# Attention and channel mix on one core: natural 128-token loads, contiguous evacuation, mixing spread over slots

## The chip, the cores and the metric

The kernel runs on one core of one Trainium2 chip. The metric is the time of one execution on the device in microseconds (us). The engines are named as in the profile: PE is TensorE with its weight loads as PEld, DVE is VectorE, ACT is ScalarE, POOL is GpSimd, and SP is SyncE, which here only issues transfers.

## The reference, cut to what matters

Eight batches of eight heads, 576 tokens, head size 64. Attention is causal by blocks of 64 tokens; its output, heads side by side, is the input x (8 x 576 x 512) of a channel mix with two mixed copies of x and three weight matrices.

```
scores = q @ k.T / 8 ; masked where block(i) < block(j)      # blocks of 64 tokens
attn   = softmax(scores) ; x = (attn @ v) as (8, 576, 512)
x_prev = x shifted by one token, zero ahead of each batch
xk = mu_k * x + (1 - mu_k) * x_prev ; xr = mu_r * x + (1 - mu_r) * x_prev
k  = relu(xk @ w_k) ; v = (k * k) @ w_v ; r = sigmoid(xr @ w_r)
out = r * v
```

## The kernel before, in words

**Loads.** `load_qk` (L82) loads q and k of a batch with SP: each of 96 partitions gets six consecutive tokens of a head, so one row of a transfer is 6 x 256 B = 1536 B. Four LD buffers hold one batch. `load_v` (L104) loads v in tiles of 128 tokens with rows of 256 B, three buffers. POOL casts q and k to bf16 (`cast_qk`, L93, tile QKN) and v to f16 (`cast_v`, L112, tile VO). The three weight matrices come as transfers that POOL issues (`load_w`, L135).

**Attention.** A pair of heads fills 128 partitions. `qk_transpose` (L145) turns q and k of a pair with six PE transposes of 96 tokens each into a PSUM tile PQK. The six pieces lie there by remainder of the token, so the copy out reads PSUM with a step of 96 elements: ACT copies q to QT (L161), DVE copies k to KT (L164). `score` (L177) computes three tiles of scores of a pair, ACT exponentiates them into E (L189), POOL zeroes masked corners (L191). `av_norm` (L218) multiplies E with v (PA) and DVE normalises (Rc L230, X L231).

**Channel mix.** `x_transpose` (L237) turns x by PE (PX), ACT copies it to XT (L259), in chunks of 512 tokens: there are 9 chunks for 8 batches. `mix` (L266) does for each of the four 128-channel groups of a chunk: POOL subtracts neighbouring tokens into DT (L272, two buffers) and mends the column where a batch begins (L277); DVE makes XK and XR (L280). `pk`, `prr` and `pv` are the three products: PK goes through ACT (relu, KR) and DVE (square, K), PR through ACT (tanh, T), PV through DVE (OV, L315), and SP stores OV.

**Order.** Work is put into slots, 13 for a batch, and the work of one slot on attention is interleaved with the units `pk`, `prr`, `pv` of an earlier chunk. `mix` of chunk b stands as a whole in slot 5 of the next batch; the units of that chunk begin two slots later. A scheduler behind this still moves instructions of one engine past each other where their inputs allow. All PSUM tiles but the scores share one pool of four buffers (`ps_m`), and every engine works through its queue in order. The lines that decide are these:

```
at(s0 + NP_ + 5, mix, b)
first = (c + 1) * NP_ + 7 if c < NCH - 1 else B * NP_ + 7
```

Of the kernel before, what the change touches and what calls it, by code (L numbers as in the profile page):

```python
# [17 lines left out]
def kernel(  # L18
# [17 lines left out]
    HP = H // 2  # L36
    CCn = C // P
    JCn = DF // P
    R = 6
    PQ = S // R  # L40
    D1 = D + 1
    CH = 512
    NCH = B * S // CH
# [16 lines left out]
    d_pool = pool("dp", 2)  # L60
    xk_pool = pool("xk", 2)
    kr_pool = pool("kr", 3)
    k2_pool = pool("k2", 1)
# [14 lines left out]
    QN, KN, QT, KT = {}, {}, {}, {}  # L78

    LD = {}  # L80

    def load_qk(b):  # L82
        for hh in range(2):
            for n, src in enumerate((q, k)):
                LD[b, n, hh] = ld_pool.tile([PQ, HP, R, D], FP, tag="ld",
                                            name="LD")
                for h in range(0, HP, 2):
                    nc.sync.dma_start(  # L88
                        LD[b, n, hh][:, h:h + 2],
                        src[b, hh * HP + h:hh * HP + h + 2].rearrange(  # L90
                            "h (p r) d -> p h r d", r=R))

    def cast_qk(b, hh, h):  # L93
        for n, (dst, tag) in enumerate(((QN, "qn"), (KN, "kn"))):
            if h == 0:
                dst[b, hh] = qk_pool.tile([PQ, R, HP, D], BF, tag=tag, bufs=2,
                                          name="QKN")
            nc.gpsimd.tensor_copy(  # L98
                dst[b, hh][:, :, h:h + 2].rearrange("p r h d -> p h r d"),
                LD[b, n, hh][:, h:h + 2])  # L100
# [15 lines left out]
    load_qk(0)  # L116
    for pr in range(HP):
        cast_qk(0, pr // 2, pr % 2 * 2)
# [24 lines left out]


    def qk_transpose(b, pr):  # L145
        if pr == 0:
            QT[b] = tr_pool.tile([P, HP, S], BF, tag="qt", name="QT")
            KT[b] = tr_pool.tile([P, HP * S + D], BF, tag="kt", name="KT")
            nc.vector.memset(KT[b][:, HP * S:], 0.0)
        for which in range(2):  # L150
            N = (QN, KN)[which][b, pr // 2]
            pst = ps_m.tile([P, CH], FP, tag="m", name="PQK")[:, :].bitcast(BF)
            view = pst[:, 0:S].rearrange("p (r t) -> p t r", r=R)
            for r in range(R):
                nc.tensor.matmul(  # L155
                    pst[:, r * PQ:(r + 1) * PQ], N[:, r, pr % 2 * 2:pr % 2 * 2 + 2, :].rearrange(
                        "p h d -> p (h d)"),
                    identb[0:PQ, 0:PQ], is_transpose=True,
                    start=(r == 0), stop=(r == R - 1))
            if which == 0:  # L160
                nc.scalar.copy(  # L161
                    QT[b][:, pr].rearrange("p (t r) -> p t r", r=R), view)
            else:
                nc.vector.tensor_copy(  # L164
                    KT[b][:, pr * S:(pr + 1) * S].rearrange(
                        "p (t r) -> p t r", r=R), view)
# [96 lines left out]

    XKR = {}

    def mix(c):  # L266
        x = XT[c]
        XK = xk_pool.tile([P, CCn, CH], F16, tag="xk", name="XK")
        XR = xk_pool.tile([P, CCn, CH], F16, tag="xr", name="XR")
        for cc in range(CCn):  # L270
            DT = d_pool.tile([P, CH], FP, tag="d", name="DT")
            nc.gpsimd.tensor_tensor(DT, x[:, cc, 1:CH + 1], x[:, cc, 0:CH],  # L272
                                    ALU.subtract)
            for b in range(B):
                t = b * S - c * CH
                if 0 <= t < CH:
                    nc.gpsimd.tensor_copy(DT[:, t:t + 1],  # L277
                                          x[:, cc, t + 1:t + 2])
            for (dst, mu) in ((XK, MUK), (XR, MUR)):
                nc.vector.scalar_tensor_tensor(  # L280
                    dst[:, cc], DT, mu[:, cc:cc + 1],
                    x[:, cc, 1:CH + 1], ALU.mult, ALU.add)
        XKR[c] = (XK, XR)
# [40 lines left out]
    def at(slot, fn, *args):  # L324
        slots.setdefault(slot, []).append((fn, args))

    for b in range(B):
        s0 = b * NP_
        order = [("s", 0, 0), ("s", 0, 1), ("s", 0, 2), ("l",)] + [
            ("s", pr, i) for pr in range(1, HP) for i in range(3)]  # L330
        for n, o in enumerate(order):
            if o[0] == "l":
                at(s0 + n, score_last, b)
            else:
                at(s0 + n, score, b, o[1], o[2])
            if b + 1 < B:
                if n == 0:
                    at(s0, load_qk, b + 1)
                if n in (3, 5, 7, 9):
                    at(s0 + n, cast_qk, b + 1, (n - 3) // 4, (n - 3) % 4)  # L340
                if n == 3 and b == 0:
                    at(s0 + n, load_w)
                if n == 4:
                    at(s0 + n, load_v, b + 1)
                if n in (8, 9, 10, 11, 12):
                    at(s0 + n, cast_v, b + 1, n - 8)
                if n in (6, 8, 10, 12):
                    at(s0 + n, qk_transpose, b + 1, (n - 6) // 2)
# [66 lines left out]
```

## Time and profile before

| what | us |
|---|---|
| median of 3 runs | 352.56 (351.91 to 353.87) |
| the profiled execution | 352.34 |
| its span | 350.6 |
| PE busy | 289.2 (83% of the span) |
| DVE busy | 212.8 (61%) |
| ACT busy | 197.0 (56%) |
| POOL busy | 161.4 (46%) |

The span is what the profiler saw of the engines; 1.74 us of the execution lie around it. The mean granted clock of PE over the span is 0.941 of full speed. The line of DMA engines in the page stands near full only in about the first sixth of the span.

### The profile page before, as it was taken

Reading aid. Unit: us, or ns where it says so; the run is one execution under the profiler, and the core shown is the slowest. Engines: PE = TensorE matmul, PEld = TensorE weight load, DVE = VectorE, ACT = ScalarE, POOL = GpSimd, SP = SyncE. Lnnn points to the kernel's source line nnn. Section 1 sums busy time; section 2 is a strip of 40 time slices with the busy share of each in tenths; the row PEclk is TensorE's granted clock in tenths of the full one; section 3 lists DMA queues with packets and bytes.
Section 4 is the critical chain, followed back from the end, with each engine's and each line's share of the span. In section 5 each row is a group of like instructions: output and inputs, shape, how many; then the busy total and the mean of one; then the engine's idle time right before and its main releaser. Section 6 shows DMA issues by size and latency. Waiting matters only on the chain.

```text
span 350.6 us, 6713 instructions
## 1 busy us (share of the span) xinstructions
PE 289.2 (83%) x2608; PEld 155.6 (44%) x2608; DVE 212.8 (61%) x366; ACT 197.0 (56%) x289; POOL 161.4 (46%) x311
## 2 busy tenths in 40 slices
PE   2750784889939996999699959997999999849995
PEld 1320652445515553555345535554455546414442
DVE  2202558982577629762967286828673974996452
ACT  2750683476716673876468636865695684315250
POOL 5811959855645754564545563665013512640000
PEclk9999995899958998999879998999899999998999
DMA  8999788095559483159104930030000100000302
GB/s 219 220 197 258 173 208 198 19 263 151 153 168 262 139 216 92 50 150 267 52 15 138 275 81 32 2 105 32 30 2 32 61 33 32 30 31 33 120 15 104
DMA packets 59184, 40.81 MB, mean 116 GB/s; under 512 B 40208, under 2 KB 54032, under 8 KB 59152
## 3 DMA queue, kind: packets, MB, share of 16 engines
q1 hardware_dynamic: 57056, 37.76, 39.6%
q0 software_dynamic: 2096, 2.62, 4.4%
q8 instruction: 20, 0.33, 0.4%
q14 instruction: 12, 0.10, 0.1%
HBM read 33.56 MB, written 9.44 MB: 123 GB/s over the span
## 4 chain that ended last, share of the span: by engine, by line
PE 56%; DVE 14%; POOL 11%; DMA 7%; issue 4%; ACT 4%; SPq 2%; POOLq 0%; DVEq 0%; ACTq 0%
PE PK L292 20%; PE PV L312 10%; PE PR L302 8%; PE PA L225 7%; POOL DT L272 6%; DMA LD<-in_k_dram 6%; DVE XR L280 5%; PE PS L185 5%; DVE XK L280 4%; PE PQK L155 3%; SPq L88 2%; DVE OV L315 2%; POOL QKN L98 2%; ACT E L189 2%; PE PX L243 2%
## 5 line engine op out<-in xcount | busy, mean ns | idle before, releaser
L189 ACT ACTIVATE E<-PS 128x1024 f16<-128x1024 f32 x96 | 97.0, 1028 | 41.0 <-PE PS L185 25.1
L292 PE MATMUL PK<-XK,WK 128*128 128x512 f16 x288 | 81.5, 427 | 18.7 <-DVE OV L315 16.7
L297 DVE TENSOR_TENSOR K<-KR 128x512 f16<-128x512 f32 x72 | 56.8, 801 | 25.7 <-ACT KR L296 25.0
L296 ACT ACTIVATE KR<-PK 128x512 f32<-128x512 f32 x72 | 43.0, 600 | 52.2 <-PE PK L292 43.9
L98 POOL CAST QKN<-LD 96x768 bf16<-96x768 f32 x64 | 58.5, 944 | 23.3 <-PE PQK L155 7.4
L312 PE MATMUL PV<-WV,K 128*128 128x512 f16 x288 | 67.8, 379 | 0.0
L191 POOL MEMSET E<- 64x128 f16 x128 | 22.9, 200 | 79.6 <-ACT E L189 73.9
L272 POOL TENSOR_TENSOR DT<-XT 128x512 f32<-128x512 f32 x36 | 42.4, 1186 | 25.4 <-DVE XR L280 14.1
L292 PEld LDWEIGHTS <-WK 128*128 128x128 f16 x288 | 27.5, 106 | 58.7 <-issue 39.0
L225 PE MATMUL PA<-VO,E 128*128 128x65 f16 x896 | 39.6, 197 | 10.5 <-DVE X L231 5.2
L315 DVE SCALAR_TENSOR_TENSOR OV<-T,PV 128x512 f32<-128x512 f32 x36 | 24.5, 680 | 35.5 <-PE PV L312 35.5
L225 PEld LDWEIGHTS <-E 128*128 128x128 f16 x896 | 35.0, 100 | 22.0 <-issue 8.3
L185 PE MATMUL PS<-QT,KT 64*128 64x512 bf16 (+4 forms) x320 | 41.9, 322 | 3.3 <-ACT E L189 3.1
L155 PE MATMUL PQK<-identb,QKN 96*128 96x96 bf16 x384 | 27.2, 223 | 18.8 <-POOL QKN L98 16.7
L280 DVE SCALAR_TENSOR_TENSOR XK<-DT,MUK,XT 128x512 f16<-128x512 f32 x36 | 30.6, 851 | 18.2 <-POOL DT L277 17.7
L312 PEld LDWEIGHTS <-K 128*128 128x128 f16 x288 | 27.2, 98 | 28.8 <-issue 1.1
L280 DVE SCALAR_TENSOR_TENSOR XR<-DT,MUR,XT 128x512 f16<-128x512 f32 x36 | 38.4, 1067 | 0.0
L302 PE MATMUL PR<-WR,XR 128*128 128x512 f16 x144 | 37.0, 382 | 1.3 <-DVE KT L164 1.3
L155 PEld LDWEIGHTS <-QKN 96*128 96x128 bf16 x384 | 22.2, 106 | 32.1 <-POOL QKN L98 23.0
L114 POOL CAST VO<-VL 128x512 f16<-128x512 f32 (+1 forms) x40 | 25.6, 655 | 21.9 <-DMA VL<-in_v_dram 17.6
L305 ACT ACTIVATE T<-PR 128x512 f32<-128x512 f32 x36 | 21.5, 596 | 21.0 <-PE PR L302 21.0
L231 DVE TENSOR_TENSOR X<-PA,Rc 128x320 f32<-128x320 f32 x64 | 31.2, 489 | 1.7
(35 smaller groups left out, 198.3 us busy)
## 6 DMA issues: line engine op xcount, KB each, us to landing
LD<-in_q_dram SPq DMA_DIRECT2D x32, 288.0 KB, 4.1
LD<-in_k_dram SPq DMA_DIRECT2D x32, 288.0 KB, 5.2
out_dram<-OV SPq DMA_DIRECT2D x36, 256.0 KB, 2.0
VL<-in_v_dram SPq DMA_DIRECT2D x32, 256.0 KB, 4.9
WK<-in_moe_w_k_dram POOLq DMA_DIRECT2D x1, 1024.0 KB, 10.1
VL<-in_v_dram SPq DMA_DIRECT2D x8, 128.0 KB, 4.1
WV<-in_moe_w_v_dram POOLq DMA_DIRECT2D x1, 1024.0 KB, 16.0
WR<-in_moe_w_r_dram POOLq DMA_DIRECT2D x1, 512.0 KB, 10.2
```

The costliest lines, as they stand in the source:

```text
L98: nc.gpsimd.tensor_copy(dst[b, hh][:, :, h:h + 2].rearrange("p r h d -> p h r d"), LD[b, n, hh][:, h:h + 2])
L155: nc.tensor.matmul(pst[:, r * PQ:(r + 1) * PQ], N[:, r, pr % 2 * 2:pr % 2 * 2 + 2, :].rearrange("p h d -> p (h d)"), identb[0:PQ, 0:PQ], i ...
L185: nc.tensor.matmul(PS[:, h, col:col + n], KT[b][rows, pr * S + kc * P: pr * S + (kc + 1) * P], QT[b][rows, pr, q0:q0 + n], start=True, sto ...
L189: nc.scalar.activation(E[:, :, i, :], PS, AF.Exp, scale=ISQ)
L225: nc.tensor.matmul(PA[:, m * D1:(m + 1) * D1], stationary(b, h, kc, m), VO[:, kc, h, 0:D1], start=(kc == 0), stop=(kc == m))
L272: nc.gpsimd.tensor_tensor(DT, x[:, cc, 1:CH + 1], x[:, cc, 0:CH], ALU.subtract)
L280: nc.vector.scalar_tensor_tensor(dst[:, cc], DT, mu[:, cc:cc + 1], x[:, cc, 1:CH + 1], ALU.mult, ALU.add)
L292: nc.tensor.matmul(ps, WK[:, cc, jc * P:(jc + 1) * P], XKR[c][0][:, cc], start=(cc == 0), stop=(cc == CCn - 1))
L296: nc.scalar.activation(KR, ps, AF.Relu)
L297: nc.vector.tensor_tensor(K2[c][:, jc], KR, KR, ALU.mult)
L302: nc.tensor.matmul(ps, XKR[c][1][:, cc, jt * P:(jt + 1) * P], WR[:, cc], start=(cc == 0), stop=(cc == CCn - 1))
L312: nc.tensor.matmul(ps, K2[c][:, jc, jt * P:(jt + 1) * P], WV[:, jc], start=(jc == 0), stop=(jc == JCn - 1))
```

## The change

Loads: q and k of a pair of heads come as four tiles of 128 tokens in rows of 256 B, one transfer for each head and tensor; the last 64 tokens of all heads come apart, q on the upper and k on the lower 64 partitions of one tile TL. There are eight LD buffers and five for v. POOL casts them to NB and TB. Transposes: eight full 128 x 128 transposes for a pair go into one PSUM bank, four more for a batch's tails; DVE alone copies them out, 1024 neighbouring elements at a time, into one tile QKT, and ACT no longer takes part. Mixing: the four subtractions of a chunk stand together (`mix_d`) with a DT for the whole chunk and one mending copy; the eight DVE instructions follow two per slot over the next four slots, all of XK first; the units of the chunk begin two slots later than before. E has two buffers instead of three.

```diff
-    qk_pool = pool("qk", 1)
+    ld_pool = pool("ld", 8)
+    vl_pool = pool("vl", 5)
+    qk_pool = pool("qk", 5)
+    tl_pool = pool("tl", 2)
     tr_pool = pool("tr", 2)
-    e_pool = pool("ep", 3)
+    e_pool = pool("ep", 2)
-    ld_pool = pool("ld", 4)
-    vl_pool = pool("vl", 3)
-    d_pool = pool("dp", 2)
+    d_pool = pool("dp", 1)
...
+    def load_qk(b, pr):
+        for n, src in enumerate((q, k)):
+            LD[b, pr, n] = ld_pool.tile([P, 4, 2, D], FP, tag="ld", name="LD")
+            for h in range(2):
+                nc.sync.dma_start(
+                    LD[b, pr, n][:, :, h],
+                    src[b, 2 * pr + h, 0:512].rearrange("(t p) d -> p t d",
+                                                        p=P))
+    def load_tail(b):
+        TL[b] = tl_pool.tile([P, H, D], FP, tag="tl", name="TL")
+        for n, src in enumerate((q, k)):
+            nc.sync.dma_start(TL[b][n * D:n * D + D],
+                              src[b, :, 512:576].rearrange("h p d -> p h d"))
+    def cast_qk(b, pr):
+        NB[b, pr] = qk_pool.tile([P, 2, 4, P], BF, tag="nb", name="NB")
+        for n in range(2):
             nc.gpsimd.tensor_copy(
+                NB[b, pr][:, n],
+                LD[b, pr, n][:, :].rearrange("p t h d -> p t (h d)"))
...
+        pst = ps_m.tile([P, CH], FP, tag="m", name="PQK")[:, :].bitcast(BF)
+        n = 8 if pr < HP else HP
+        for i in range(n):
+            src = (NB[b, pr][:, i // 4, i % 4] if pr < HP
+                   else NB[b, HP][:, i * P:(i + 1) * P])
+            nc.tensor.matmul(pst[:, i * P:(i + 1) * P], src, identb,
+                             is_transpose=True, start=(i == 0),
+                             stop=(i == n - 1))
+        if pr < HP:
+            nc.vector.tensor_copy(
+                QKT[b][:, :, pr * S:pr * S + 512],
+                pst.rearrange("p (n t) -> p n t", n=2))
...
-    def mix(c):
+    def mix_d(c):
         x = XT[c]
+        DT = d_pool.tile([P, CCn, CH], FP, tag="d", name="DT")
...
         for cc in range(CCn):
+            nc.gpsimd.tensor_tensor(DT[:, cc], x[:, cc, 1:CH + 1],
+                                    x[:, cc, 0:CH], ALU.subtract)
+        for b in range(B):
+            t = b * S - c * CH
+            if 0 <= t < CH:
+                nc.gpsimd.tensor_copy(DT[:, :, t:t + 1], x[:, :, t + 1:t + 2])
+    def mix(c, n, cc):
+        nc.vector.scalar_tensor_tensor(
+            XKR[c][n][:, cc], XKR[c][2][:, cc], (MUK, MUR)[n][:, cc:cc + 1],
+            XT[c][:, cc, 1:CH + 1], ALU.mult, ALU.add)
...
-        at(s0 + NP_ + 5, mix, b)
-    at(B * NP_ + 5, mix, NCH - 1)
+        sm = s0 + NP_ + 5
+        for c in ((b,) if b < B - 1 else (b, b + 1)):
+            sm = s0 + NP_ + 5 + 6 * (c - b)
+            at(sm, mix_d, c)
+            for i in range(8):
+                at(sm + 1 + i // 2, mix, c, i // 4, i % 4)
...
-        first = (c + 1) * NP_ + 7 if c < NCH - 1 else B * NP_ + 7
+        first = (c + 1) * NP_ + 9
```

On POOL, at the start of the program, the order of the casts and of the three weight transfers (WK, WR, WV) before is this; QKN is a cast of q or k, VO one of v, E the zeroing of masked corners:

```order
11 L98 CAST QKN<-LD 96x2x6x64 x8
12 L136 DMA WK<-in_moe_w_k_dram 128x4x1024
13 L114 CAST VO_116<-VL 128x8x64 x3
14 L191 MEMSET E 64x2x64 x4
15 L137 DMA WR<-in_moe_w_r_dram 128x4x512
16 L98 CAST QKN<-LD 96x2x6x64
17 L138 DMA WV<-in_moe_w_v_dram 128x8x512
```

And now:

```order
11 L98 CAST NB<-LD 128x512 x2
12 L104 CAST TB<-TL 128x512
13 L146 DMA WK<-in_moe_w_k_dram 128x4x1024
14 L98 CAST NB<-LD 128x512 x2
15 L147 DMA WR<-in_moe_w_r_dram 128x4x512
16 L98 CAST NB<-LD 128x512 x2
17 L200 MEMSET E 64x2x64 x4
18 L148 DMA WV<-in_moe_w_v_dram 128x8x512
```

The first weight transfer was issued behind all eight casts of batch 0; now it is issued behind the casts of its first pair and the tail.

On DVE, in the middle of the program where a chunk is mixed while the next batch's attention runs, the order before is this; XK and XR are the mixed copies, OV the product that goes out, Rc and X the normalisation, KT a copy of transposed k:

```order
143 L257 COPY XT<-XT 128x4
144 L280 SCALAR_TENSOR_TENSOR XK<-DT,MUK,XT 128x512
145 L280 SCALAR_TENSOR_TENSOR XR<-DT,MUR,XT 128x512
146 L280 SCALAR_TENSOR_TENSOR XK<-DT,MUK,XT 128x512
147 L315 SCALAR_TENSOR_TENSOR OV<-T,PV 128x512
148 L280 SCALAR_TENSOR_TENSOR XR<-DT,MUR,XT 128x512
149 L280 SCALAR_TENSOR_TENSOR XK<-DT,MUK,XT 128x512
150 L280 SCALAR_TENSOR_TENSOR XR<-DT,MUR,XT 128x512
151 L280 SCALAR_TENSOR_TENSOR XK<-DT,MUK,XT 128x512
152 L280 SCALAR_TENSOR_TENSOR XR<-DT,MUR,XT 128x512
153 L230 RECIPROCAL Rc<-PA 128x5
154 L315 SCALAR_TENSOR_TENSOR OV<-T,PV 128x512
```

And now, with QKT as the copy of transposed q and k:

```order
149 L290 SCALAR_TENSOR_TENSOR XK<-DT,MUK,XT 128x512 x4
150 L290 SCALAR_TENSOR_TENSOR XR<-DT,MUR,XT 128x512
151 L324 SCALAR_TENSOR_TENSOR OV<-T,PV 128x512
152 L290 SCALAR_TENSOR_TENSOR XR<-DT,MUR,XT 128x512
153 L239 RECIPROCAL Rc<-PA 128x5
154 L290 SCALAR_TENSOR_TENSOR XR<-DT,MUR,XT 128x512
155 L240 TENSOR_TENSOR X<-PA,Rc 128x5x64
156 L290 SCALAR_TENSOR_TENSOR XR<-DT,MUR,XT 128x512
157 L239 RECIPROCAL Rc<-PA 128x5
158 L240 TENSOR_TENSOR X<-PA,Rc 128x5x64
159 L324 SCALAR_TENSOR_TENSOR OV<-T,PV 128x512
160 L168 COPY QKT<-PQK 128x2x512
```

The four XK now stand first and together, the last three XR between one OV and two normalisations that stood behind all eight.

On POOL, where a chunk in the middle is mixed, the order before is this (VO is a cast of v, DT the subtraction and its mending copy):

```order
113 L272 TENSOR_TENSOR DT<-XT 128x512 x2
114 L277 COPY DT<-XT 128x1 x2
115 L191 MEMSET E 64x2x64
116 L272 TENSOR_TENSOR DT<-XT 128x512
117 L277 COPY DT<-XT 128x1
118 L191 MEMSET E 64x2x64
119 L272 TENSOR_TENSOR DT<-XT 128x512
120 L277 COPY DT<-XT 128x1
```

And now:

```order
112 L200 MEMSET E 64x2x64 x3
113 L104 CAST TB<-TL 128x512
114 L282 TENSOR_TENSOR DT<-XT 128x512 x4
115 L119 CAST VO_120<-VL 128x8x64
116 L287 COPY DT<-XT 128x4
```

The four subtractions now stand together, and one cast of v stands between them and the mending copy.

## Rows read from the trace of the kernel before

**Rows 1.** Stretches of the span: start:end, length, busy us (instructions) by engine, clock, DMA, GB/s

```profile
0.00:44.00 44.00, 21.12 (x243) 12.91 (x244) 11.99 (x31) 19.02 (x23) 22.99 (x51) 1.00 0.99 213
44.00:60.00 16.00, 9.78 (x128) 6.62 (x125) 11.08 (x16) 10.73 (x15) 11.81 (x23) 0.78 0.94 222
60.00:102.00 42.00, 33.25 (x321) 18.09 (x319) 29.31 (x46) 23.55 (x35) 28.12 (x51) 0.91 0.54 142
102.00:211.00 109.00, 99.05 (x933) 53.81 (x932) 70.42 (x128) 67.88 (x100) 57.73 (x107) 0.92 0.53 146
211.00:280.00 69.00, 65.65 (x635) 35.28 (x632) 46.35 (x84) 47.46 (x69) 27.81 (x61) 0.96 0.11 36
280.00:316.00 36.00, 29.67 (x230) 15.41 (x231) 28.36 (x46) 15.85 (x27) 12.95 (x20) 1.00 0.09 33
316.00:346.50 30.50, 30.50 (x135) 13.47 (x133) 14.62 (x23) 12.54 (x21) 0.00 (x0) 0.95 0.16 61
```

**Rows 2.** Timeline, 127.5 to 139 us: start, us, engine, line, out<-in, [idle before <-releaser]

```profile
127.91 2.04 POOL L272 TENSOR_TENSOR DT<-XT 128x512 f32<-128x512 f32 x2 [1.37 <-ACT XT L259]
130.11 0.75 DVE L280 SCALAR_TENSOR_TENSOR XK<-DT,MUK,XT 128x512 f16<-128x512 f32 x1 [2.08 <-POOL DT L277]
...
133.11 0.68 PE L155 MATMUL PQK<-identb,QKN 96*128 96x96 bf16 x12
...
134.00 1.42 POOL L272 TENSOR_TENSOR DT<-XT 128x512 f32<-128x512 f32 x1 [0.51 <-DVE XR L280]
134.44 1.52 DVE L280 SCALAR_TENSOR_TENSOR XR<-DT,MUR,XT 128x512 f16<-128x512 f32 x1
...
138.18 1.37 PE L292 MATMUL PK<-XK,WK 128*128 128x512 f16 x3 [2.99 <-DVE OV L315]
```

**Rows 3.** The seven stretches with a lowered clock; columns as in Rows 1

```profile
53.00:64.00 11.00, 6.94 (x47) 3.58 (x47) 9.90 (x14) 2.59 (x5) 10.14 (x19) 0.54 0.66 148
97.00:108.00 11.00, 6.31 (x36) 3.02 (x36) 7.41 (x13) 2.53 (x5) 3.50 (x9) 0.53 0.70 200
138.00:142.00 4.00, 3.83 (x10) 1.19 (x10) 2.48 (x6) 0.89 (x2) 0.00 (x0) 0.57 0.17 66
172.00:180.00 8.00, 6.01 (x28) 2.16 (x27) 4.98 (x10) 2.47 (x4) 0.57 (x4) 0.57 0.09 34
210.00:214.00 4.00, 3.53 (x24) 1.79 (x25) 2.26 (x5) 1.32 (x2) 0.20 (x1) 0.58 0.20 70
247.00:251.00 4.00, 4.00 (x14) 1.19 (x13) 1.97 (x5) 2.77 (x4) 0.20 (x1) 0.57 0.17 66
315.00:320.00 5.00, 4.49 (x14) 1.70 (x14) 5.00 (x9) 3.01 (x6) 0.00 (x0) 0.66 0.14 52
```

**Rows 4.** Groups by line: operation, count, busy us, mean ns, idle before by releaser

```profile
L189 ACT ACTIVATE E<-PS 128x1024 f16<-128x1024 f32 x96 | 97.0, 1028 | 41.0 <-PE PS L185 25.1 <-PE PA L225 14.0 <-POOL QKN L98 0.9
L280 DVE SCALAR_TENSOR_TENSOR XR<-DT,MUR,XT 128x512 f16<-128x512 f32 x36 | 38.4, 1067 | 0.0
L280 DVE SCALAR_TENSOR_TENSOR XK<-DT,MUK,XT 128x512 f16<-128x512 f32 x36 | 30.6, 851 | 18.2 <-POOL DT L277 17.7
L164 DVE COPY KT<-PQK 128x576 bf16<-128x576 bf16 x32 | 24.0, 750 | 12.6 <-PE PQK L155 12.6
L140 DVE TENSOR_SCALAR WV<-WV 128x4096 f16<-128x4096 f16 x1 | 1.2, 1227 | 0.7 <-DMA WV<-in_moe_w_v_dram 0.7
```

**Rows 5.** DMA packets of 72 to 79 us, loads of q and k

```profile
DMA packets 1376, 1.96 MB, mean 280 GB/s; under 512 B 114, under 2 KB 1374, under 8 KB 1374
```

**Rows 6.** DMA packets of 106 to 110 us, mostly loads of v

```profile
DMA packets 2760, 1.12 MB, mean 280 GB/s; under 512 B 2436, under 2 KB 2759, under 8 KB 2759
```

**Rows 7.** DMA queues of 20 to 28 us: packets, MB, share of 16 engines

```profile
q0 software_dynamic: 1168, 1.26, 91.2%
q1 hardware_dynamic: 1169, 0.30, 28.1%
```

**Rows 8.** Timeline of SP's queue: start, us, line, transfers issued

```profile
46.34 0.94 SPq L88 DMA_DIRECT2D LD<-in_k_dram  x2
```

More of the change, by code (lines that the diff above doesn't have):

```diff
@@ L38 @@
     JCn = DF // P
-    R = 6
-    PQ = S // R
+    SP_ = HP * S + D
     D1 = D + 1
@@ L76, with cast_tail @@
     E4s = [consts.tile([P, H, P], F16, name=f"EL{i}") for i in range(2)]
[L78 to L97, printed above, removed]
-            nc.gpsimd.tensor_copy(
-                dst[b, hh][:, :, h:h + 2].rearrange("p r h d -> p h r d"),
-                LD[b, n, hh][:, h:h + 2])
+    LD, NB, TL, QKT = {}, {}, {}, {}
+    def load_qk(b, pr):
[14 more added lines that the diff above has]
+        for n in range(2):
+            nc.gpsimd.tensor_copy(
+                NB[b, pr][:, n],
+                LD[b, pr, n][:, :].rearrange("p t h d -> p t (h d)"))
+    def cast_tail(b):
+        NB[b, 4] = tl_pool.tile([P, C], BF, tag="tb", name="TB")
+        nc.gpsimd.tensor_copy(NB[b, 4],
+                              TL[b][:, :].rearrange("p h d -> p (h d)"))
     VL = {}
@@ L114, in cast_v @@
         nc.gpsimd.tensor_copy(VOs[b % 2][0:n, sc, :, 0:D], VL[b, sc][0:n])
-    load_qk(0)
     for pr in range(HP):
-        cast_qk(0, pr // 2, pr % 2 * 2)
+        load_qk(0, pr)
+        if pr == 0:
+            load_tail(0)
+    load_v(0)
+    for pr in range(HP):
+        cast_qk(0, pr)
+        if pr == 0:
+            cast_tail(0)
     for i in range(2):
@@ L145, in qk_transpose @@
     def qk_transpose(b, pr):
[L146 to L166, printed above, removed]
+        if b not in QKT:
+            QKT[b] = tr_pool.tile([P, 2, SP_], BF, tag="qkt", name="QKT")
+            nc.vector.memset(QKT[b][:, 1, HP * S:], 0.0)
+        pst = ps_m.tile([P, CH], FP, tag="m", name="PQK")[:, :].bitcast(BF)
[10 more added lines that the diff above has]
+                pst.rearrange("p (n t) -> p n t", n=2))
+        else:
+            nc.vector.tensor_copy(
+                QKT[b][:, :, 0:HP * S].rearrange(
+                    "p n (a s) -> p n a s", s=S)[:, :, :, 512:S],
+                pst[:, 0:HP * P].rearrange("p (a n t) -> p n a t", n=2, t=D))
     PIECES = [
@@ L186, in score @@
                     PS[:, h, col:col + n],
-                    KT[b][rows, pr * S + kc * P: pr * S + (kc + 1) * P],
-                    QT[b][rows, pr, q0:q0 + n], start=True, stop=True)
+                    QKT[b][rows, 1, pr * S + kc * P: pr * S + (kc + 1) * P],
+                    QKT[b][rows, 0, pr * S + q0:pr * S + q0 + n], start=True, stop=True)
         nc.scalar.activation(E[:, :, i, :], PS, AF.Exp, scale=ISQ)
@@ L200, in score_last @@
                     PS[:, h, pr * D:pr * D + D],
-                    KT[b][rows, pr * S + 512: pr * S + 640],
-                    QT[b][rows, pr, 512:576], start=True, stop=True)
+                    QKT[b][rows, 1, pr * S + 512: pr * S + 640],
+                    QKT[b][rows, 0, pr * S + 512:pr * S + 576], start=True, stop=True)
         nc.scalar.activation(
@@ L264 @@
     XKR = {}
-    def mix(c):
+    def mix_d(c):
         x = XT[c]
+        DT = d_pool.tile([P, CCn, CH], FP, tag="d", name="DT")
         XK = xk_pool.tile([P, CCn, CH], F16, tag="xk", name="XK")
         XR = xk_pool.tile([P, CCn, CH], F16, tag="xr", name="XR")
+        XKR[c] = (XK, XR, DT)
         for cc in range(CCn):
[L271 to L283, printed above, removed]
+            nc.gpsimd.tensor_tensor(DT[:, cc], x[:, cc, 1:CH + 1],
[8 more added lines that the diff above has]
+            XT[c][:, cc, 1:CH + 1], ALU.mult, ALU.add)
     K2, T = {}, {}
@@ L335 @@
                 at(s0 + n, score, b, o[1], o[2])
[L336 to L348, printed above, removed]
+        if b + 1 < B:
+            for pr in range(HP):
+                at(s0 + pr, load_qk, b + 1, pr)
+                at(s0 + (4, 5, 7, 8)[pr], cast_qk, b + 1, pr)
+                at(s0 + (7, 8, 9, 10)[pr], qk_transpose, b + 1, pr)
+            at(s0 + 3, load_tail, b + 1)
+            at(s0 + 9, cast_tail, b + 1)
+            at(s0 + 11, qk_transpose, b + 1, HP)
+            at(s0 + 4, load_v, b + 1)
+            for sc in range(5):
+                at(s0 + (6, 9, 10, 11, 12)[sc], cast_v, b + 1, sc)
+        if b == 0:
+            at(s0 + 3, load_w)
         for pr in range(HP):
@@ L367 @@
     qk_transpose(0, 0)
+    qk_transpose(0, HP)
     for pr in range(1, HP):
-        at(pr - 1, qk_transpose, 0, pr)
+        slots.setdefault(pr - 1, []).insert(0, (qk_transpose, (0, pr)))
     nu = 0
```

3 lines of the change are left out of this document (1 added, 2 removed).

## The prediction

> **What bounds the kernel now.** I read the stretches of the span first, then the timeline around one stall, then the stretches of low clock, then the groups and the DMA packets. The stretches [rows 1] show three regimes. Up to 44 us PE is busy 21.1 of 44 us while the DMA engines are at 0.99: batch 0, the weights and batch 1's q and k come in, and the transfers set the time. From 44 to 60 us batch 1's attention runs alone, with PE busy 9.8 of 16 us. From 60 to 346.5 us PE has work for the channel mix beside the attention, and no other engine is near full: DVE, the next, has 70.4 of 109 us between 102 and 211 us. So PE's stream sets the time there, and what can be won is its idle time and its slow clock. The idle time from 60 to 346.5 us is length less busy in the five rows: 8.8 + 10.0 + 3.4 + 6.3 + 0 = 28.5 us. The timeline [rows 2] shows where it lies: a chunk's mixing begins on POOL at 127.9, takes POOL and DVE in turns (each waits for the other), and PE stands idle for 2.99 us until PK can begin at 138.18, ten microseconds after the first subtraction. The last row's releaser is OV, not XK: products wait on DVE behind the mixing and hold PSUM buffers. After such gaps the granted clock is near half in seven stretches [rows 3]. Busy time times one less the clock is what they lost: 3.2 + 3.0 + 1.6 + 2.6 + 1.5 + 1.7 + 1.5 = 15.1 us, all of it behind 53 us.
>
> **Mixing, the part that pays.** DVE's eight instructions do not go away, and POOL's four subtractions stay. What changes is the turn-taking: the subtractions go back to back, at 1.02 us each (2.04 for two) [rows 2], 4.1 us for four; the new order puts one cast between them and the mending copy, an instruction of the same size with one input less and so at most another 1.02, and XK waits about 5 us for POOL. That wait is a new one at the head of DVE's queue, and behind it stand OV, two normalisations and QKT. PE can go on until four PSUM buffers wait for DVE; in the new order it has about four such products there, with PX and PR, which ACT empties, in between. Behind the wait, DVE needs 4 x 0.75 for XK and then alternates XR with what PE waits for. PE's gap was about 3 us for a middle chunk; it can become 0, and at worst stays 3.5. I take 1.5 for each of eight chunks, 12 us instead of 28.5, nearer the lower end because three XR now stand behind an OV and a normalisation, and because the units of a chunk begin two slots later, behind work that needs no XK. The last two chunks, whose sixteen mixings in one burst fill DVE (28.4 of 36 us up to 316, PE 29.7 [rows 1]), now have six slots between them.
>
> **The clock.** With gaps half as long, I take 3 of the 15.1 us to stay; bounds 0 and 15.1.
>
> **The first attention.** From 44 to 60 us PE idles 6.2 us. Behind the change two more slots of attention fall ahead of the first PK; ten exponentials at 1.03 [rows 4] outlast PE's work there, so I keep 3.5 us idle and gain 2.7.
>
> **Transposes on PE.** Twelve for a pair take 0.68 us [rows 2], 57 ns apiece. Eight of 128 columns take 0.45 us if they cost the same apiece, 0.60 if by columns; four tails for a batch 0.23 to 0.30. A batch goes from 2.7 to 2.0 to 2.7 us. I take 2 us less over seven batches (bounds 0 and 5).
>
> **Evacuation on DVE.** ACT loses 32 copies; ACT is not last in the long stretch, so this is worth nothing by itself. DVE's copy reads 576 elements with a step in 0.75 us [rows 4]; the new one reads 1024 neighbours. No row shows that form. By L164's rate it takes 1.33 us; by the cheapest DVE row, 4096 f16 elements in 1.23 us from SBUF [rows 4], 0.31. I take 1.33, as L164 has the same engine, source and type. DVE then has, for a chunk, 70.4/3 = 23.5 less 4 x 0.75 plus 4 x 1.33 plus half of one for the tails: 26.5 us. PE's need for a chunk is 99.05 less some 7.4 lost to the clock between 102 and 211, over three: 30.5. DVE stays under it by 4 us, about as much as its new wait, which is why I leave PE 1.5 us a chunk rather than none. The cover is thin.
>
> The Trainium skill (VectorE: DVE Perf Modes, section The perf-mode tier table) says that a copy with a PSUM operand can run at up to twice the base rate; its walkthrough asks for 16-bit neighbours, which the new copy has and the old one had not. By it the copy would be about half of 1.33 us, and an estimate from that leaves DVE at the old 23.5 us a chunk and the forecast some 4 us lower. The row of L164 agrees with the base rate; no run shows the other.
>
> **Loads.** Bytes stay, rows of q and k go from 1536 to 256 B. From 72 to 79 us q and k moved at 280 GB/s [rows 5]; from 106 to 110 us, with 2436 of 2760 packets below 512 B, also 280 [rows 6]. So the rows cost nothing where the queue has the engines to itself. Against this stands the Trainium skill (DMA: Bandwidth & Descriptors, section Specifications), by which transfers below 512 B miss the line rate; the trace disagrees at 256 B, and the rule is a rival below. Beside the weights it is different: from 20 to 28 us both queues moved the same number of packets, 1168 and 1169, but 1.26 and 0.30 MB [rows 7]. WK is now issued behind three casts instead of eight, so the weights pass while half of batch 0 is still to come, at 256 B a turn. That moves batch 0 back, not the sum: the same bytes must land before batch 1's scores. Before, 0.85 MB of batch 1's v came in by then (213 GB/s x 44 us is 9.4 MB, of which 2.6 weights and 5.9 q, k and batch 0's v), now v comes behind q and k: 3 us less at 280 GB/s. With two E buffers the third pair of batch 0 waits for v; v lands ahead of batch 1's q and k, so this lies beside their loading. I take 2 us gained, bounds 5 lost and 5 gained. SP issues 23 loads for a batch instead of 13, at 0.47 us [rows 8] 5 us more in 36, and an OV that waits behind them has three buffers; in the long stretch the DMA engines have half their time free. POOL's casts get shorter, its order is in the wait above.
>
> **Sum.** Span 350.6; idle 34.7 to 15.5 is -19.2; clock 15.1 to 3 is -12.1; transposes -2; loads -2: 315.3. The profiled execution took 1.74 us more than its span, 352.34, which is 0.22 below the median: 317. I forecast 318 us. With each term at its bounds (gaps 0 to 24, clock 0 to 9 with them, transposes, loads) its own range is 303 to 333.
>
> **Rivals.**
> - The stall moves. DVE waits for POOL's whole block, PE fills its four buffers and stands as long as before, and the clock falls each time. For it: releaser OV in the last row [rows 2], and 5 us at the head of DVE's queue. Against: only four buffers' worth of PE work is needed to cover it. Only loads, transposes and the first attention gain, 2 + 2 + 2.7 + 1.5 of clock: 344. Chance 0.14.
> - Short rows are slow, at half the rate. Batches 0 and 1 have 4.7 MB of q and k, at 140 instead of 280 GB/s 17 us more ahead of batch 1; later they hide (2.36/140 and as much v and out at 280 make 25 us a chunk, under 30.5). 335. Against: rows 6. Chance 0.06.
> - DVE becomes the bound: slower. POOL's casts and subtractions now run beside the mixing all the time, and an instruction of DVE beside a subtraction took 1.52 instead of 0.75, a subtraction beside it 1.42 instead of 1.02 [rows 2]. Eight mixings at 1.52 instead of 0.96, the mean of XK's 0.85 and XR's 1.07 [rows 4], add 4.5 to 26.5, and the wait at its queue's head grows to five times 1.42, 7: 38 us a chunk, 1.7 more than the 36.3 of before (109/3), over eight chunks 13.6, less 8.2 of the first rival's gains: 358. It decides from 36.3 + 1 us a chunk. Chance 0.07.
> - The mixing is not what holds PE, and nothing moves but details: 350 to 352. Chance 0.03.
>
> **Chances.** The forecast has 0.65, still better (below 303, no gap and DVE's copy short) 0.05, and the rivals the rest. The range 303 to 344 holds the forecast, the slow rows and most of the first rival, a little over 0.8. A measurement of this kernel tells about 0.5% from no change. Faster by more than that: 0.65 + 0.05 + 0.14 + 0.06 = 0.90; within it 0.03; slower 0.07.
>
> **What would show it.** Right: DT in blocks of four with XK behind them, PE's idle time between the first PK and the last under 16 us, one or two stretches of low clock instead of seven, DMA at 280 GB/s with q and k alone, first PK near 54 us. Wrong: PE idle 3 us at each chunk with OV or X as releaser (first rival); DMA well below 280 GB/s with 256 B rows alone (second); DVE above 33 us a chunk (third); batch 1's scores later than 49 us would break the term of the loads.

## The result, and the profile after

The change makes the kernel faster, by less than half of what was forecast: 337.53 us (median of 4, 336.97 to 339.67) against 353.22 us of the kernel before in the same session (351.91 to 353.91). The ratio is 0.957, its 95% interval 0.952 to 0.963; the forecast of 318 us would be 0.90. The time lies inside the range of 303 to 344 us, near its upper end, where the rival stood by which the stall only moves.

The profiled execution took 337.89 us, 14.5 less than that of before. The stretches of the kernel after, with the columns of [rows 1]; the first three end where terms of the prediction end, the other four serve for comparisons below:

```profile
0.00:44.00 44.00, 20.34 (x168) 11.20 (x169) 11.14 (x28) 12.21 (x13) 18.47 (x44) 1.00 0.99 192
44.00:60.00 16.00, 11.22 (x156) 7.92 (x151) 5.25 (x16) 10.79 (x15) 10.49 (x21) 0.88 0.97 220
60.00:332.30 272.30, 254.35 (x2192) 131.86 (x2192) 180.41 (x329) 155.69 (x230) 111.78 (x231) 0.96 0.41 104
...
0.00:57.00 57.00, 30.88 (x312) 18.80 (x313) 15.30 (x42) 21.07 (x25) 26.10 (x61) 0.97 0.98 198
57.00:75.00 18.00, 13.75 (x109) 6.68 (x108) 12.60 (x23) 9.12 (x11) 11.46 (x25) 0.72 0.94 211
75.00:280.00 205.00, 192.21 (x1849) 102.42 (x1850) 136.78 (x260) 129.01 (x186) 94.04 (x202) 0.98 0.44 110
280.00:336.10 56.10, 49.08 (x247) 23.08 (x244) 32.80 (x51) 19.50 (x36) 9.15 (x9) 1.00 0.15 57
```

PE's idle time from 44 us on is length less busy in the second and third row, 4.8 + 17.9 = 22.7 us, where it was 34.7 before and was forecast at 15.5. The clock is lowered in five stretches instead of seven:

```profile
46.00:50.00 4.00, 3.35 (x57) 3.09 (x57) 2.17 (x6) 0.47 (x1) 1.71 (x3) 0.57 1.12 252
59.00:70.00 11.00, 8.80 (x54) 4.05 (x55) 8.61 (x13) 3.16 (x4) 7.37 (x15) 0.53 0.97 220
97.00:101.00 4.00, 4.00 (x19) 1.73 (x18) 4.00 (x10) 1.02 (x1) 0.60 (x2) 0.57 0.16 61
131.00:135.00 4.00, 3.90 (x12) 1.18 (x12) 3.88 (x9) 0.00 (x0) 0.49 (x1) 0.57 0.17 66
165.50:169.00 3.50, 2.69 (x7) 0.99 (x7) 3.46 (x9) 0.00 (x0) 0.00 (x0) 0.51 0.50 138
```

Busy time times one less the clock is 1.4 + 4.1 + 1.7 + 1.7 + 1.3 = 10.2 us, against 15.1 [rows 3] and 3 forecast.

What PE still waits for, in the view of waits (engine, line, releaser: us in total, times, longest):

```profile
PE PQK L164 <- POOL NB L98: 17.5, 8, 6.4
PE PV L321 <- DVE OV L324: 12.4, 6, 2.6
PE PA L234 <- POOL VO L119: 5.6, 2, 5.1
```

The second line is the old stall in a new place. In the timeline around the chunk at 131 us (it answers to [rows 2]) it reads so:

```profile
121.28 4.03 POOL L282 TENSOR_TENSOR DT<-XT 128x512 f32<-128x512 f32 x4 [1.37 <-ACT XT L268]
...
124.16 1.89 PE L321 MATMUL PV<-WV,K 128*128 128x512 f16 x8
...
125.81 0.19 POOL L287 COPY DT<-XT 128x4 f32<-128x4 f32 x1
...
126.04 3.75 DVE L290 SCALAR_TENSOR_TENSOR XK<-DT,MUK,XT 128x512 f16<-128x512 f32 x4 [3.21 <-POOL DT L287]
...
127.88 0.60 ACT L314 ACTIVATE T<-PR 128x512 f32<-128x512 f32 x1 [0.45 <-PE PR L311]
...
128.49 0.19 PE L234 MATMUL PA<-VO,EL 128*128 128x65 f16 x1
...
129.72 0.74 DVE L290 SCALAR_TENSOR_TENSOR XR<-DT,MUR,XT 128x512 f16<-128x512 f32 x1
...
130.38 0.67 DVE L324 SCALAR_TENSOR_TENSOR OV<-T,PV 128x512 f32<-128x512 f32 x1
...
131.10 3.33 PE L321 MATMUL PV<-WV,K 128*128 128x512 f16 x8 [2.42 <-DVE OV L324]
```

The PV that ends at 126.05 is ready for DVE just as the four XK start. OV stands behind them and one XR, and starts at 130.38. PE has three more products for the other places of the PSUM pool (PA, PR, PA), which end at 128.68; then it waits 2.42 us for OV. The place of PR has been empty since 128.48, when ACT's T had read it out, but the next PV waits for the place of the PV before it, which only OV empties.

One chunk earlier DVE itself stands still in front of that row: the PV there had ended at 91.26, DVE waits for POOL until 93.38, and OV starts behind two XK at 95.38. PE's gap is 2.22 us.

```profile
93.38 2.08 DVE L290 SCALAR_TENSOR_TENSOR XK<-DT,MUK,XT 128x512 f16<-128x512 f32 x2 [5.01 <-POOL DT L287]
95.38 0.67 DVE L324 SCALAR_TENSOR_TENSOR OV<-T,PV 128x512 f32<-128x512 f32 x1
```

Two prices that had no row, or only a neighbour's, can now be read. The new copy out of PSUM, as a group by line (columns as in [rows 4]):

```profile
L168 DVE COPY QKT<-PQK 128x1024 bf16<-128x1024 bf16 x32 | 22.0, 687 | 28.9 <-PE PQK L164 28.3
```

And the packets from 37 to 40 us, when rows of 256 B of q and k moved alone:

```profile
DMA packets 2825, 0.70 MB, mean 234 GB/s; under 512 B 2825, under 2 KB 2825, under 8 KB 2825
```

### The profile page after: what moved, and what is told of

It reads as the page before. It is cut to its first block, busy times and chain, and to the rows that moved or that the text cites. A ratio compares the mean times of both kernels' runs of the same rounds, so it can differ in the third digit from the quotient of the medians.

```text
span 336.1 us, 6653 instructions
## 1 busy us (share of the span) xinstructions
PE 285.9 (85%) x2512; PEld 151.0 (45%) x2512; DVE 197.5 (59%) x374; ACT 178.7 (53%) x257; POOL 140.7 (42%) x295
## 5 line engine op out<-in xcount | busy, mean ns | idle before, releaser
L321 PE MATMUL PV<-WV,K 128*128 128x512 f16 x288 | 71.4, 394 | 13.0 <-DVE OV L324 12.4
L301 PE MATMUL PK<-XK,WK 128*128 128x512 f16 x288 | 71.8, 387 | 2.1 <-DVE OV L324 2.1
L306 DVE TENSOR_TENSOR K<-KR 128x512 f16<-128x512 f32 x72 | 53.1, 746 | 14.9 <-ACT KR L305 14.4
L98 POOL CAST NB<-LD 128x512 bf16<-128x512 f32 x64 | 43.3, 689 | 30.3 <-DMA LD<-in_k_dram 12.7
L194 PE MATMUL PS<-QKT 64*128 64x512 bf16 (+4 forms) x320 | 43.2, 320 | 5.4 <-ACT E L198 5.2
L282 POOL TENSOR_TENSOR DT<-XT 128x512 f32<-128x512 f32 x36 | 37.3, 1065 | 20.0 <-ACT XT L268 6.9
L164 PE MATMUL PQK<-identb,NB 128*128 128x128 bf16 x256 | 25.8, 248 | 17.5 <-POOL NB L98 17.5
L301 PEld LDWEIGHTS <-WK 128*128 128x128 f16 x288 | 25.3, 99 | 32.0 <-issue 8.8
L168 DVE COPY QKT<-PQK 128x1024 bf16<-128x1024 bf16 x32 | 22.0, 687 | 28.9 <-PE PQK L164 28.3
L164 PEld LDWEIGHTS <-NB 128*128 128x128 bf16 x256 | 17.8, 110 | 29.1 <-POOL NB L98 23.3
```

Source lines behind the costliest of these rows:

```text
L98: nc.gpsimd.tensor_copy(NB[b, pr][:, n], LD[b, pr, n][:, :].rearrange("p t h d -> p t (h d)"))
L164: nc.tensor.matmul(pst[:, i * P:(i + 1) * P], src, identb, is_transpose=True, start=(i == 0), stop=(i == n - 1))
L194: nc.tensor.matmul(PS[:, h, col:col + n], QKT[b][rows, 1, pr * S + kc * P: pr * S + (kc + 1) * P], QKT[b][rows, 0, pr * S + q0:pr * S + q0 ...
L282: nc.gpsimd.tensor_tensor(DT[:, cc], x[:, cc, 1:CH + 1], x[:, cc, 0:CH], ALU.subtract)
L301: nc.tensor.matmul(ps, WK[:, cc, jc * P:(jc + 1) * P], XKR[c][0][:, cc], start=(cc == 0), stop=(cc == CCn - 1))
L306: nc.vector.tensor_tensor(K2[c][:, jc], KR, KR, ALU.mult)
```

## The experiments

**Which part of the change pays.** One kernel is that of before with the new `mix_d`, `mix`, slots and units; the other is the changed kernel with the old ones.

```diff
 # mix only (from before)           # loads only (from after)
-def mix(c): ...                    +def mix(c): ...
+def mix_d(c): ...                  -def mix_d(c): ...
+def mix(c, n, cc): ...             -def mix(c, n, cc): ...
+first = (c + 1) * NP_ + 9          +first = (c + 1) * NP_ + 7 if ... 
```

> The kernel before with the new mixing alone; loads, transposes, evacuation and the three E buffers as before. If the changed kernel's gain is all the mixing's and its loads cost the 5 us by which its first PK comes later (65.4 instead of 60.2 us), this kernel has its first PK near 61 us and is about 3 to 5 us faster than the changed one: 333 to 335 us. If the shorter evacuation and the fewer transposes bring part of the gain, it is slower than the changed one: 339 to 345 us.

> The changed kernel with the old mixing: four single subtractions in turn with DVE, all in one slot, units two slots earlier. If loads, transposes and evacuation cost about 3 to 5 us by themselves: 353 to 358 us, with the old gaps of 3 us at each chunk. If they bring a part of the gain: 340 to 350 us.

Measured: mixing only 334.98 us (ratio 0.951, 0.942 to 0.959), loads only 352.87 us (1.000, 0.995 to 1.004). So all of the gain is the mixing's. The loads, transposes and copies together bring nothing that can be told from no change, neither of the two amounts expected for them.

**The wait for POOL at the head of DVE's queue.** The 3.21 us in the XK line above might be what pushes OV back. Here XK and XR read x one token back instead of DT (another result); POOL still makes DT, but nobody waits for it.

```diff
-XKR[c][n][:, cc], XKR[c][2][:, cc], (MUK, MUR)[n][:, cc:cc + 1],
+XKR[c][n][:, cc], XT[c][:, cc, 0:CH], (MUK, MUR)[n][:, cc:cc + 1],
```

> The changed kernel with XK and XR made from x one token back in place of the difference DT (so the mixing's values are other ones); POOL still makes DT, and nothing reads it. DVE's eight instructions stay, only their wait for POOL goes. Theory (the wait of 3 to 5 us at the head of DVE's queue makes PE's gap of about 2.2 us a chunk and the slow clock behind it): the gaps fall under 0.7 us, the slow clock behind 80 us goes, and the time falls by 12 to 20 us to 318 to 326. Rival (the burst of eight on DVE is too long by itself, wherever it begins): the gaps stay above 1.5 us and the time falls by less than 6 us, to 332 to 338.

Measured: 338.83 us (0.962, 0.956 to 0.969). Taking the wait away alone gains nothing. XK starts about 4 us earlier behind the start of POOL's block, but now beside it, and four XK take 5.5 us where four took 3.75 in the chunk at 131 us; OV comes no earlier and the gap stays. So this run does not show that the wait costs nothing: it exchanges the wait for a longer row, and only a run without the block can tell what the two are worth together. From its timeline:

```profile
87.97 4.92 POOL L282 TENSOR_TENSOR DT<-XT 128x512 f32<-128x512 f32 x4 [2.63 <-ACT XT L268]
...
88.95 5.51 DVE L290 SCALAR_TENSOR_TENSOR XK<-XT,MUK 128x512 f16<-128x512 f32 x4
...
95.05 0.68 DVE L324 SCALAR_TENSOR_TENSOR OV<-T,PV 128x512 f32<-128x512 f32 x1
...
95.77 1.89 PE L321 MATMUL PV<-WV,K 128*128 128x512 f16 x8 [2.16 <-DVE OV L324]
```

**The late start.** The weights' transfers were held until the last cast of batch 0's q and k.

```diff
 def load_w():
+    GT = NB[0, 3][:, 1, 3]
+    nc.gpsimd.tensor_copy(WK[:, 0, 0:1], GT[:, 0:1])   # and WR, WV
```

> The changed kernel with one column of each weight tile first written from the last cast of batch 0's q and k, so that no weight transfer is issued before batch 0's q and k are in. Theory (weights ahead of batch 0's 256 B rows starve them, and SP stands in its queue so that batch 1's loads begin only at 31 us): PE no longer idles from 13 to 19 us, batch 1's loads begin before 28 us and the first PK comes 3 to 6 us earlier, time 331 to 335. Rival (rows of 256 B move at some 225 to 243 GB/s instead of 280, and the bytes ahead of batch 1 set the time whatever their order): the first PK moves by less than 2 us, time 335.5 to 338.

Measured: 336.24 us (0.956, 0.949 to 0.963), first PK at 66.42. The weights that go ahead of batch 0 are not what costs: PE's idle time from 13 to 19 us falls from 6.0 to 1.6 us, but from 19 to 44 us it grows from 10.6 to 16.4.

**Order on DVE.** The other way is to take OV out from behind the row, whatever the row waits for. The scheduler had put the row of XK and XR together; now each mixing instruction is kept behind what the program writes ahead of it on DVE, with no wait added. It was done to the changed kernel and to the kernel with the mixing alone.

```diff
-nc.vector.scalar_tensor_tensor(XKR[c][n][:, cc], ...)
+tc.keep_in_program_order(nc.vector.scalar_tensor_tensor(XKR[c][n][:, cc], ...))
```

> The changed kernel with each mixing instruction kept, on DVE's queue alone, behind what the program writes ahead of it (no wait is added): the two mixings of a slot then stand between OV, X and QKT instead of four XK and one XR in a row ahead of the OV. Theory (the burst of XK ahead of OV is what still holds PE at each chunk, 2.0 to 2.4 us apiece and a low clock behind it): PE's idle time before PV put down to OV falls from 12.4 us to under 4, the low-clock stretches after 80 us go, and the time falls by 7 to 12 us to 326 to 331 us. Rival (PE is short of buffers or work there in any order; the stop moves to another instruction): idle before PV moves to PA, PQK or PK and the time stays at 335 to 339 us.

> The kernel before with the new mixing alone (335.0 us), its mixing kept in the written order on DVE as in the run before this one. Theory of the burst: PE's waits for DVE at the chunks (PV for OV and X, PQK for OV: 15.8 us in all) fall under 8 and the time to 324 to 329 us; it then stays 1 to 4 us ahead of the same edit on the changed kernel, since its first PK comes 3 us earlier. Rival (order does not matter): 333 to 337 us.

Measured: 323.93 us (0.922, 0.917 to 0.927) and 324.99 us (0.924, 0.920 to 0.928). The theory holds, and the gain, 13.6 us as the times stand and some 12 by the ratios, is at the upper end of what it gave. No wait of PV for OV is left, and from 75 to 280 us PE is busy 202.90 of 205 us at full clock, where it was 192.21 at 0.98. In the timeline of the first one OV comes ahead of XK, and PE goes from PA to PV without a gap:

```profile
91.02 0.69 DVE L324 SCALAR_TENSOR_TENSOR OV<-T,PV 128x512 f32<-128x512 f32 x1 [2.92 <-PE PV L321]
...
93.10 2.07 DVE L290 SCALAR_TENSOR_TENSOR XK<-DT,MUK,XT 128x512 f16<-128x512 f32 x2 [0.47 <-POOL DT L287]
...
93.42 0.19 PE L234 MATMUL PA<-VO,EL 128*128 128x65 f16 x1
93.45 1.89 PE L321 MATMUL PV<-WV,K 128*128 128x512 f16 x8
```

**POOL's block.** The subtractions are left out, the mixing reads x one token back (another result), the scheduler's order stays free.

```diff
-nc.gpsimd.tensor_tensor(DT[:, cc], x[:, cc, 1:CH + 1], x[:, cc, 0:CH], ALU.subtract)
-nc.gpsimd.tensor_copy(DT[:, :, t:t + 1], x[:, :, t + 1:t + 2])
-XKR[c][n][:, cc], XKR[c][2][:, cc], (MUK, MUR)[n][:, cc:cc + 1],
+XKR[c][n][:, cc], XT[c][:, cc, 0:CH], (MUK, MUR)[n][:, cc:cc + 1],
```

> The changed kernel with POOL's subtractions left out and the mixing reading x shifted by one token in their place (a different result). Theory of the burst, in which POOL's block makes it longer by sharing access (four XK took 5.5 us beside the block, 3.0 to 3.7 without): four XK take 3.0 us and start 4 us earlier, OV comes 2 us or more earlier, PE's gaps at the chunks fall from 2.0-2.4 us to 1 or less: 328 to 333 us. Rival (the gap is not DVE's): 335 to 339 us, as with the subtractions made but not read (338.8 us).

Measured: 311.87 us (0.887, 0.884 to 0.890), 16 us below the better end of what I expected. Beside the kernel whose subtractions were made and not read, 27 us are due to POOL's block alone. The chunk that answers to the last two timelines reads so here:

```profile
83.28 2.73 DVE L281 SCALAR_TENSOR_TENSOR XK<-XT,MUK 128x512 f16<-128x512 f32 x4
84.37 1.89 PE L312 MATMUL PV<-WV,K 128*128 128x512 f16 x8
85.93 1.10 DVE L281 SCALAR_TENSOR_TENSOR XR<-XT,MUR 128x512 f16<-128x512 f32 x1
86.95 0.67 DVE L315 SCALAR_TENSOR_TENSOR OV<-T,PV 128x512 f32<-128x512 f32 x1
88.73 1.89 PE L312 MATMUL PV<-WV,K 128*128 128x512 f16 x8
```

The PV ends at 86.26, OV starts 0.7 us later, and the next PV begins without a wait. The XK group in that kernel, in this one, and the stretch of 75 to 280 us in this one:

```profile
L290 DVE SCALAR_TENSOR_TENSOR XK<-XT,MUK 128x512 f16<-128x512 f32 x36 | 46.9, 1348 | 0.0
```

```profile
L281 DVE SCALAR_TENSOR_TENSOR XK<-XT,MUK 128x512 f16<-128x512 f32 x36 | 26.4, 782 | 0.0
```

```profile
75.00:280.00 205.00, 205.00 (x1915) 109.81 (x1914) 151.19 (x287) 137.42 (x203) 66.30 (x167) 1.00 0.45 115
```

By the means, four XK in a row take 3.1 us and not 5.4; the row starts as soon as x is there and ends before PE has used up its buffers, though OV still stands behind it. In the changed kernel, where XK comes after the block, its mean is 901 ns: there the wait ahead of the row, 2.4 to 5.0 us at the six chunks between 75 and 280 us, is most of what the block costs, and the row is only some 0.5 us longer. PE has no idle time at all for 205 us. The block also costs at the start: without it the first PK came at 62.41 at full clock, with it at 65.42 in the changed kernel and 66.59 with the order kept, both at half.

**The mixing computed without a block on POOL.** In one kernel DVE subtracts; in the other ACT scales x by mu into a tile AT, and DVE adds the shifted x times (1 - mu). In both, DVE's part of the mixing is kept in order. Cut to the lines that matter:

```diff
 # DVE subtracts
-nc.gpsimd.tensor_tensor(DT[:, cc], ...)
+tc.keep_in_program_order(nc.vector.tensor_tensor(DT[:, cc], ...))
 # ACT scales
+nc.scalar.activation(AT[:, cc], x[:, cc, 1:CH + 1], AF.Copy, scale=(MUK, MUR)[n][:, cc:cc + 1])
+nc.vector.scalar_tensor_tensor(X[:, cc], XT[c][:, cc, 0:CH], (MVK, MVR)[n][:, cc:cc + 1],
+                               AT[:, cc], ALU.mult, ALU.add)     # MVK = 1 - MUK
+nc.vector.tensor_copy(X[:, :, t:t + 1], AT[:, :, t:t + 1])        # where a batch begins
```

> The changed kernel with the subtractions moved from POOL to DVE (two, then their two XK, in the program's order, as in the run with the mixing kept in order). Leaving the subtractions out altogether gave 311.9 us, keeping the order with them on POOL 323.9. If what POOL's block costs beyond the order is its sharing with DVE and its place in POOL's queue, DVE pays 36 x some 0.75 us = 27 us of its own time (194 to 221 of some 315 us busy), beside PE's work, and XK takes 0.78 us as without POOL, not 0.88: 313 to 319 us. If DVE's time is what counts now, its extra 3 us a chunk come back as waits of PE: 320 to 330 us.

> The changed kernel without subtractions: ACT scales x by mu into a tile of its own (72 copies of some 0.6 us, 43 us more on ACT: 179 to 222 us busy), and DVE adds the shifted x times (1 - mu) to it, as many mixings as before, kept in order; POOL has no block. If the cost was POOL's block, the time goes to 312 to 317 us, near the 311.9 us of the run that leaves the subtractions out. If ACT's up to four scalings in a row ahead of an exp are paid by PE (its scores waited 5 to 6 us for ACT already), 318 to 328 us.

Measured: DVE 328.17 us (0.930, 0.924 to 0.936), no faster than with the block on POOL and the order kept (the intervals overlap); ACT 319.10 us (0.900, 0.890 to 0.911). DVE's time counts: beside XK at 782 ns its subtractions take 729 ns, and PE waits again for OV, QKT and X (idle from 75 to 280 us 6.5 us, where it was 2.1 with the order kept). Over the span idle time and clock loss come out even with that kernel, 43.7 + 2.9 against 41.4 + 6.0 us; the 3.4 us between the two profiled executions lie in PE's busy time, and no row says why. ACT has the room: it goes from 179 to 219 us busy.

**Three more on that version:** with the loads, transposes and copies of before; with a third buffer for E; and with the order on DVE free again.

```diff
-e_pool = pool("ep", 2)
+e_pool = pool("ep", 3)
 # the other: keep_in_program_order taken away again
```

> The kernel with ACT's scaling (319.1 us), but with the loads, transposes and evacuations of the kernel before (1536 B rows, 96-token transposes, Q's evacuation on ACT). If the loads' part of the change is worth nothing, as with the old mixing (352.9 against 353.5 us) and with the order kept (323.9 against 325.0), 317 to 322 us: PE gains some 5 us up to its 75th microsecond and loses it later. If ACT counts now (16 us more of it in Q's evacuations, to some 236 us busy), 322 to 330 us, and the new evacuation is then worth that much beside this mixing.

> The kernel with ACT's scaling and three buffers for E in place of two (the change took one away). PE's scores waited 6.7 us for E's exp and mask. If those waits are the buffers', they go and the time falls 2 to 5 us to 314 to 317 us; if they are the exp's own length between a score and the use of its PSUM buffer, nothing changes: 317 to 321 us.

> The kernel with ACT's scaling (319.1 us), its mixing no longer kept in the written order: three XK and a small copy stand ahead of an OV again, but no POOL block beside them. If the order and POOL's block are two causes of one gap, so that without the block three XK of 0.78 us end before PE runs out of buffers (as in the run without subtractions, where PE had no gap between 75 and 280 us), 315 to 321 us. If the order costs by itself, without POOL's part, PE's gaps at the chunks come back at 1 us or more apiece: 325 to 332 us.

Measured: 320.10 us (0.909, 0.903 to 0.915), 321.31 us (0.913, 0.906 to 0.919), and 315.63 us (0.897, 0.892 to 0.901). The old loads make no difference here either, and the waits for E are not the buffers'. The last is 22 us ahead of the changed kernel and, but for the run without subtractions, the fastest of all. In its stretches no idle time is left from 75 to 280 us, as without subtractions; nearly all that is left lies ahead of it:

```profile
57.00:75.00 18.00, 13.45 (x128) 6.93 (x128) 13.68 (x27) 13.07 (x18) 9.28 (x20) 0.81 1.05 211
75.00:280.00 205.00, 204.98 (x1935) 110.17 (x1932) 150.47 (x298) 173.69 (x268) 66.93 (x169) 1.00 0.49 115
```

| | order free | mixing kept in order |
|---|---|---|
| POOL subtracts | 337.5 (the change) | 323.9 |
| ACT scales, no block | 315.6 | 319.1 |

So the order and the block are two causes of one gap: with the block the order is worth 13.6 us (10.0 with the old loads), without it nothing that can be told (the intervals of the lower row overlap). The rows were measured in four sessions, in which the kernel before took 351.7 to 354.0 us.

## Why the prediction was wrong

**What held.** PE's stream sets the time and the mixing's place holds it up; that gain is real and is all there is. DT stands in blocks of four with XK behind. Batch 1's scores came no later (44.65 us), so that bound of the loads' term held.

**The step that failed: "PE can go on until four PSUM buffers wait for DVE; in the new order it has about four such products there, with PX and PR, which ACT empties, in between", and so 1.5 us a chunk.** The prediction saw the wait for POOL and the four buffers, but counted products and not time, and took it that PE stops only when all four wait for DVE. The trace shows PE stopped at 128.68 for the one buffer whose turn it is, with PR's empty. The three products between one PV and the next take 126.05 to 128.68, 2.6 us; DVE needs 4.3 us from the same moment until it starts OV, and 0.7 more until the buffer is free. That is 2.4 us of gap, as measured; the six gaps between 75 and 280 us come to 12.4 us, 2.1 apiece. The wait of about 5 us at the head of DVE's queue, which I had named as the new price, was there, 2.4 to 5.0 us at these six chunks, and it is part of the cause; taking it away alone did not help, because DVE's row is longer beside POOL. I had a figure for that, 1.52 for 0.75 us, but only in the rival of a slower kernel. To keep the order takes 13.6 us off, to have ACT scale in place of the block 22; 19.5 us were missing to the forecast.

**A second step failed with it: "With gaps half as long, I take 3 of the 15.1 us to stay".** No row gave that size. The idle time behind 60 us fell to 17.9 of 28.5 us, and the clock's loss stayed at 10.2 of 15.1, about in step. Of the 10.2, 4.7 us lie behind three of the six gaps; the other 5.5 lie at 46 to 50 and 59 to 70 us, in and just behind the first attention, already more than the 3 left in all.

**The sum, term by term.** Idle time from 44 us on: 34.7 - 22.7 = 12.0 us gained, 19.2 forecast. Clock: 4.9 gained, 12.1 forecast. Transposes: 0 gained, 2 forecast; eight of 128 columns take 0.62 us against 0.68 for twelve, the upper of the two prices I gave, and the tails come on top. Loads: about 1 us lost, 2 gained forecast; idle up to 44 us is 23.7 instead of 22.9. With 1.2 us more of PE's work at full clock (busy time times clock by microseconds, 274.2 before and 275.4 now), 12.0 + 4.9 - 0.8 - 1.2 = 14.9 is near the 14.5 us between the two profiled executions.

**First PK near 54 us** was wrong by 11 us. Before, it came at 59.98 us, and two slots of attention were put ahead of it; in no run here did it come before 59.60. 62.4 us is what the run without block shows for the new slots; the rest is PE standing 2.76 us at 60.44 for a cast that waits in POOL's queue behind the block, and the half clock behind it:

```profile
57.79 2.04 POOL L282 TENSOR_TENSOR DT<-XT 128x512 f32<-128x512 f32 x2
59.77 0.61 POOL L98 CAST NB<-LD 128x512 bf16<-128x512 f32 x1
60.32 0.19 POOL L287 COPY DT<-XT 128x4 f32<-128x4 f32 x1
60.44 0.61 PE L164 MATMUL PQK<-identb,NB 128*128 128x128 bf16 x4 [2.76 <-POOL NB L98]
...
65.42 1.90 PE L301 MATMUL PK<-XK,WK 128*128 128x512 f16 x4
```

**The copy out of PSUM** was taken at 1.33 us, between bounds of 0.31 and 1.33; it takes 0.687. By the Trainium skill (VectorE: DVE Perf Modes, section The perf-mode tier table) a copy from PSUM runs at up to twice the base rate, an estimate of half of 1.33 us, and the trace agrees. The 4 us that I would have gained by it are not to be seen: beside the new mixing the old copies took no longer (334.98 us).

**The rows of 256 B** move at 234 GB/s instead of 280 [rows 5]. The rule of the Trainium skill (DMA: Bandwidth & Descriptors, section Specifications) that transfers below 512 B miss the line rate, which I set aside on a stretch of v, holds for q and k by a sixth, far from the half of the rival. The old loads are in fact ahead at the start: with ACT's scaling PE had run 42.6 us of work at full clock (busy time times clock, by microseconds) by 75 us with them, and 38.9 with the new ones. They lose it later, idle 6.2 instead of 2.4 us from 75 to 280 us. So in these two executions the zero of this part is two effects of some 4 us that cancel.

**Rivals.** "The stall moves" (344 us, 0.14) had the mechanism right and only the size wrong, 2.1 us a gap on the mean instead of 3; it was worth more than I gave it. The time of "short rows are slow" (335) came out nearest of all, by luck: its rate did not come, and with the old rows the same mixing took 334.98 us. DVE as the bound was wrong for this change, but its figure of XK beside a subtraction came back when the wait was taken away. That the mixing does not hold PE is excluded.

## What to carry to other kernels

A product's buffer is free when the engine that empties it gets to it, so compare in microseconds what PE has left in its other buffers with the longest wait and row of work that stand ahead of that engine's emptying instruction; a count of buffers does not answer it, and a buffer that another engine has emptied does not help when it is not its turn. Removing a wait tells little when the work then runs beside what it waited for. Read in the built order where a scheduler has pulled spread instructions together again, and pin them or shorten the row. Two engines that slow each other belong in the sum of the likeliest case. Part of the work may be cheaper on a third engine that has time left, as the scaling was on ACT, even if it is more work in all.

## What the hardware showed

XK takes two inputs from SBUF, and beside POOL's subtractions it took 1348 ns on the mean against 782 without them, while DT took 1310 ns in the same kernel and 1065 in the changed one, where XK waits for it. The Trainium skill (SBUF — State Buffer, section Who interferes with whom) says that a DVE instruction with two SBUF inputs contends with a GpSimd instruction that reads SBUF, and calls the port pair that they share an exclusive lock. The trace agrees that they contend; if each XK had to let a whole DT pass, it would take an estimated 0.78 + 1.07 = 1.85 us, and the median of that kernel's 36 XK is 1.52.

The granted clock did not fall after every gap: it fell to about half after those at 94, 129 and 164 us, and stayed at 1.00 in the stretches of 198 to 201, 231 to 233 and 259 to 261 us, with 2.1, 1.5 and 1.6 us of idle time. The three gaps that it fell after were the longest, 2.22, 2.42 and 2.56 us; in the run without the wait it fell after two of 2.43 and 2.25 us and not after one of 2.16. So few gaps do not show that the length decides.
